# The conditioning vector on the ScalarE queue, and two more k-tiles of q whose shift enters as a bias, in an adaLN transformer block

## The chip, the cores and the metric

The kernel runs on one core of a Trainium2 chip. The metric is device time in microseconds of the whole program, the median of several executions. The profiler's span, which the timelines below use, is 2.2 to 2.6 µs shorter than the device time of the same execution.

## The reference, cut to what matters

```python
# x: [1, 2048, 1024], 32 heads, F = 3584, all bf16
mod = silu(c) @ w_mod                    # six vectors of 1024: sa, ca, ga, sb, cb, gb
h = layernorm(x) * (1 + ca) + sa         # ca: scale, sa: shift
q, k, v = split(h @ wqkv)                # then linear attention, wo, residual with ga
...
h = layernorm(x) * (1 + cb) + sb         # then a SwiGLU block, residual with gb
```

What is changed is only how the first quarter of the rows ("chunk 0": four x tiles of 128 rows) gets from x to q. The contraction over the 1024 input features is done in eight k-tiles of 128.

## The kernel before

The loads are queued on SyncE in the order in which TensorE will want them. `wca` and `wsa` hold the columns of `w_mod` that give the scale and the shift. Each comes in two halves, and half 1 of `wsa` (k-tiles 4 to 7) comes first.

```python
P.dma("c", CS8[0:NDT, :], cv8)                       # 2 KB, queue "sp"
for st in range(4):
    P.dma("x0_%d" % st, XRES[:, st, :], xv[:, st, :])   # x tiles 0..3, 256 KB each
ca_load(0); wq_load(0, 2); ca_load(1); wq_load(2, 2)    # 1 MB, 512 KB, 1 MB, 512 KB
sa_load(1)                                           # 1 MB: shift weights of k-tiles 4..7
wq_load(4); wq_load(5); wq_load(6); wq_load(7)
sa_load(0)                                           # shift weights of k-tiles 0..3
```

The four x tiles are normalised one by one. VectorE takes the statistics of tiles 0, 1 and 3. ScalarE takes those of tile 2, in two passes over it (`act_stats(2)`); `m2` copies them into the form that the rest uses.

```python
act_stats(2)                       # ScalarE: sum, then sum of squares
s0_[0](); s0_[1](); s1_[0](); s0_[2](); ln1_rstd1(0)          # VectorE from here on
s1_[1](); s1_[2](); ln1_rstd1(1)
ln1_xn(0); tile_transposes(0); warm(5, bank=3)
s3_[0]()
ln1_xn_act(1); tile_transposes(1); warm(1, bank=3)            # tile 1 on ScalarE
m2[1](); m2[0](); neg_rstd(2)                                 # needs ScalarE's passes
s3_[1](); s3_[2](); ln1_rstd1(3)
ln1_xn(2); ln1_xn(3)
mod_sc(WCA, 8, range(2)); fin_ca(0, 2); tile_transposes(2, 3)
h0_first(0, "dve"); h0_first(1, "dve")
```

The q projection of chunk 0 keeps seven output tiles (`nt`) open in seven PSUM banks and goes through the k-tiles one or two at a time. K-tiles 0 to 3 get only their scale before the matmul. Their shift enters q as a bias (`bias_mm`: 32 matmuls of one column), and is added to the tiles afterwards, for k. K-tiles 4 to 7 get scale and shift at once, so they need `wsa` first.

```python
mod_sc(WCA, 8, range(4, 8)); fin_ca(4, 4)
for nt in range(7):
    if nt == 6:
        mod_sc(WSA, 0, range(4, 6)); fin_sa(4, 2)     # 16 matmuls: first use of wsa
        for dt in (4, 5): h0_scale(dt)                # VectorE: scale and shift
    q_part(nt, qb[nt], (2, 3))
mod_sc(WSA, 0, range(6, 8)); fin_sa(6, 2)
for dt in (6, 7): h0_scale(dt)
act_stats(4)
for dt in (4, 5, 6):
    for nt in range(7): q_part(nt, qb[nt], (dt,))
... # k-tile 7; between its matmuls mod_sc(WSA, 0, range(4)) and bias_mm()
ln1_xn(5); ln1_xn(4); th_dma(5); th_dma(4)            # chunk 1: normalise, transpose by DMA
... # the eighth output tile
for dt in range(4): h0_shift(dt)
```

Of the kernel before, what the change touches and what calls it, by code (L numbers as in the profile page):

```python
# [93 lines left out]


class _Op:
    __slots__ = ("idx", "eng", "fn", "deps", "signaled", "count", "semkey", "waits", "ninc", "tag")

    def __init__(self, idx, eng, fn, semkey, ninc, tag):
        self.idx = idx  # L100
        self.eng = eng
        self.fn = fn
        self.semkey = semkey
        self.ninc = ninc
        self.deps = {}
        self.signaled = False
        self.count = None
        self.waits = []
        self.tag = tag


def _is_ap(v):
# [6 lines left out]
class _Prog:  # L119
# [7 lines left out]
        self.dma_ops = []  # L127

    def add(self, eng, fn, reads=(), writes=(), lane=None, ninc=1, tag=None):
        if eng in self.COMPUTE:  # L130
            semkey = eng
        else:
            assert lane is not None
            semkey = "lane:" + lane
        op = _Op(len(self.ops), eng, fn, semkey, ninc, tag)
        deps = op.deps

        def deps_add(d):
            if d is op:
                return  # L140
            k = d.semkey
            if k not in deps or deps[k].idx < d.idx:
                deps[k] = d

        banks = set()
        for ap, is_w in [(a, False) for a in reads] + [(a, True) for a in writes]:
            space, ivs = _ap_intervals(ap)
            if space == "dram":
                continue
            if space == "ps":  # L150
                for a, b in ivs:
                    for bank in range(a // PSUM_BANK_BYTES, (b - 1) // PSUM_BANK_BYTES + 1):
                        banks.add(bank)
                continue
            for a, b in ivs:
                self.seg.access(a, b, op, is_w, deps_add)
        for bank in banks:
            st = self.excl.get(bank)
            if st:
                for e2, d in st.items():  # L160
                    if e2 != eng:
                        deps_add(d)
            self.excl[bank] = {eng: op}
        self.ops.append(op)
        self.by_eng.setdefault(eng, []).append(op)
        if eng not in self.COMPUTE:
            self.dma_ops.append(op)
        return op

# [37 lines left out]
    def resolve(self):  # L207
        for op in self.ops:
            for d in op.deps.values():
                d.signaled = True  # L210
        for op in self.ops:
            if op.eng not in self.COMPUTE and op.fn is not None:
                op.signaled = True
        counters = {}
        for op in self.ops:
            if op.signaled:
                c = counters.get(op.semkey, 0) + (op.ninc if op.eng in self.COMPUTE else 16 * op.ninc)
                counters[op.semkey] = c
                op.count = c
        known = {}  # L220
        snaps = {}
        for op in self.ops:
            kn = known.setdefault(op.eng, {})
            waits = []
            for k, d in sorted(op.deps.items(), key=lambda kv: kv[1].idx):
                if kn.get(k, 0) >= d.count:
                    continue
                waits.append((k, d.count))
                for kk, vv in snaps[d.idx].items():
                    if kn.get(kk, 0) < vv:  # L230
                        kn[kk] = vv
                if kn.get(k, 0) < d.count:
                    kn[k] = d.count
            op.waits = waits
            if op.signaled:
                sn = dict(kn)
                if op.eng in self.COMPUTE:
                    sn[op.semkey] = op.count
                snaps[op.idx] = sn
        return counters  # L240

    def emit(self, sems, engines):
        for eng, ops in self.by_eng.items():
            deco = engines[eng]

            def body(e, ops=ops, eng=eng):
                for op in ops:
                    for k, v in op.waits:
                        e.wait_ge(sems[k], v)
                    if op.fn is None:  # L250
                        continue
                    r = op.fn(e)
                    if op.signaled:
                        if eng in self.COMPUTE:
                            r.then_inc(sems[op.semkey], op.ninc)
                        else:
                            rs = r if isinstance(r, (list, tuple)) else [r]
                            assert len(rs) == op.ninc
                            for ri in rs:
                                ri.then_inc(sems[op.semkey], 16)  # L260

            deco(body)


def bass_adaLN_cond__linear_attn_block__swiglu_ffn__prompt_kernel(
# [22 lines left out]
    with ExitStack() as es:  # L288
# [104 lines left out]

        P = _Prog()

        P.dma("c", CS8[0:NDT, :], cv8)
        for st in range(4):
            P.dma("x0_%d" % st, XRES[:, st, :], xv[:, st, :])

# [3 lines left out]
        def sa_load(p):  # L403
            P.dma("wsa%d" % p, WSA[:, :, 512 * p:512 * p + 512], wmv[:, :, 512 * p:512 * p + 512])

        def wq_load(i, n=1):
            P.dma("wq%d" % i, WQK[:, i:i + n, 0:D], wqkvv[:, i:i + n, 0:D])
# [2 lines left out]
        wq_load(0, 2)  # L410
        ca_load(1)
        wq_load(2, 2)
        sa_load(1)
        wq_load(4)
        wq_load(5)
        wq_load(6)
        wq_load(7)
        sa_load(0)
# [97 lines left out]
        def fin_sa(m, n, cast=False):  # L516
            if cast:
                P.dve("tensor_copy", out=MODTMP[:, m:m + n], in_=PS[:, 0, m:m + n])
            P.dve("tensor_copy", out=MODCOL[:, 1, m:m + n], in_=PS[:, 0, m:m + n])

        def h0_shift(dt):
            P.dve("tensor_scalar", out=HT[:, 0, dt, :], in0=HT[:, 0, dt, :], scalar1=MODCOL[:, 1, dt:dt + 1],
                  scalar2=None, op0=ALU.add)

        def bias_mm():
            for nt in range(NDT):
                for dt in range(4):
                    P.pe("matmul", out=PS[:, 0, 16 + nt:17 + nt], lhsT=WQK[:, dt, nt * 128:(nt + 1) * 128],
                         rhs=MODTMP[:, dt:dt + 1], start=False, stop=(dt == 3), skip_group_check=True)
            P.dve("tensor_copy", out=BIASQ[:], in_=PS[:, 0, 16:24])  # L530

        def t_view(dt, n=1):
# [81 lines left out]
        s3_[0]()  # L614
        ln1_xn_act(1)
        tile_transposes(1)
        warm(1, bank=3)
        m2[1]()
        m2[0]()
        neg_rstd(2)  # L620
# [65 lines left out]

        def k_group(ch, nt):
            buf, bank = ch % 2, next_bank()
            for i, dt in enumerate((4, 5, 6, 7, 0, 1, 2, 3) if ch == 0 else range(NDT)):
                P.pe("matmul", out=PS[:, bank, :], lhsT=WQK[:, dt, D + nt * 128:D + (nt + 1) * 128],  # L690
                     rhs=HT[:, buf, dt, :], start=(i == 0), stop=(i == 7))
            phi_evac(bank, (ch, nt))
# [36 lines left out]
        def q_phase_chunk0(side):  # L729
# [9 lines left out]
                    q_part(nt, qb[nt], dts)  # L739
            mod_sc(WCA, 8, range(4, 8))  # L740
            fin_ca(4, 4)
            for nt in range(7):
                if nt == 6:
                    mod_sc(WSA, 0, range(4, 6))
                    fin_sa(4, 2)
                    for dt in (4, 5):
                        h0_scale(dt)
                q_part(nt, qb[nt], (2, 3))
            mod_sc(WSA, 0, range(6, 8))
            fin_sa(6, 2)  # L750
            for dt in (6, 7):
                h0_scale(dt)
            act_stats(4)
            for dt in (4, 5, 6):
                for nt in range(7):
                    q_part(nt, qb[nt], (dt,))
            for nt in range(7):
                if nt == 0:
                    mod_sc(WSA, 0, range(4))
                    fin_sa(0, 4, True)  # L760
                    for f in ln_ops[1]:
                        f()
                    ln1_rstd1(5)
                if nt == 4:
                    bias_mm()
                q_part(nt, qb[nt], (7,))
            for f in act_mv_ops(4):
                f()
            neg_rstd(4)
            ln1_xn(5)  # L770
            ln1_xn(4)
            th_dma(5)
            th_dma(4)
            q_phi = lambda nt: phi_evac(qb[nt] if nt < 7 else 0, PQT[:, nt, 0:512], bias=BIASQ[:, nt:nt + 1])
            for i, dt in enumerate(range(NDT)):
                P.pe("matmul", out=PS[:, 0, :], lhsT=WQK[:, dt, 896:1024], rhs=HT[:, 0, dt, :], start=(i == 0),
                     stop=(i == 7))
            for dt in range(4):
                h0_shift(dt)
            for nt in range(8):  # L780
                q_phi(nt)
                for f in side.get(nt, []):
                    f()
# [389 lines left out]
```

## Time and profile before

| | |
|---|---|
| device time, three runs before the prediction | 836.26, 836.29, 834.89 µs |
| span of the profiled run | 833.0 µs, TensorE busy 99% |
| first projection matmul | 12.67 µs |
| TensorE waits for `wsa` | 0.61 µs, its matmuls start at 20.08 µs |
| first matmul of k | 30.80 µs |

These lines are the head of the page of the kernel before.

```profile
span 833.0 us, 10031 instructions
PE 821.9 (99%) x4053; PEld 379.9 (46%) x4132; DVE 301.7 (36%) x659; ACT 196.2 (24%) x335; POOL 43.6 (5%) x56
PE 94%; DVE 3%; DMA 1%; SPq 1%; issue 1%; ACT 0%; DVEq 0%; ACTq 0%
```

TensorE is the bottleneck. Note 4053 matmuls against 4132 weight loads (PEld): 79 matmul records are missing from this trace. So a milestone of TensorE is read here from the weight loads, which are complete. A weight load is pulled ahead to the start of the matmul before it, so the first matmul starts when the second weight load does. The prediction's 12.88 µs for the first projection matmul is the first matmul record of this trace; by the weight loads it was 12.67.

The chain of waits of the kernel before, in order of time (start, length, what):

```profile
0.79 0.40 SPq L178
1.24 0.36 SPq L178
...
8.79 11.24 DMA wsa<-in_w_mod_dram
20.08 0.57 PE ps L178 x16
...
31.87 10.74 PE ps L178 x49
```

The chain says that nothing before 20.08 µs set the time except the queue of loads that ends in `wsa`.

The next lines are TensorE's timeline of the kernel before (start, length, tiles written and read, count, and in brackets the idle time before it with what ended it). 512-column matmuls start every 0.216 µs, one-column ones every 0.025 µs; the length of a merged line contains the pipeline of its last matmul.

```profile
17.10 2.54 PE L178 MATMUL ps<-ht,wqk 128*128 128x512 bf16 x11
20.08 0.55 PE L178 MATMUL ps<-siluc,wsa 128*128 128x1 bf16 x16 [0.44 <-DMA wsa<-in_w_mod_dram]
20.50 0.59 PE L178 MATMUL ps<-ht,wqk 128*128 128x512 bf16 x2
20.93 0.54 PE L178 MATMUL ps<-siluc,wsa 128*128 128x1 bf16 x16
...
27.62 0.94 PE L178 MATMUL ps<-modtmp,wqk 128*128 128x1 bf16 x32
```

The last matmul ahead of `wsa` starts at 19.26 µs, so the next could have started at 19.48; it starts at 20.08. Measured from start to start the wait is 0.61 µs; the 0.44 in the bracket leaves out the pipeline's drain. "Wait" below is start to start beyond the 0.216 µs pace.

Two views of the fill belong together. First ScalarE's timeline, then VectorE's, both of the kernel before.

```profile
6.28 1.06 ACT L178 ACTIVATE ht<-xres 128x1024 bf16<-128x1024 bf16 x1 [3.68 <-DMA xres<-in_A_x_dram]
7.24 0.19 ACT L178 ACTIVATION_READ_ACCUMULATOR ht<-xres 128x1 f32 x1
7.46 1.06 ACT L178 ACTIVATE ht<-xres 128x1024 bf16<-128x1024 bf16 x1
8.42 0.19 ACT L178 ACTIVATION_READ_ACCUMULATOR ht<-xres 128x1 f32 x1
```

```profile
7.21 0.54 DVE L178 TENSOR_SCALAR xres<-xres,mv,rstd 128x1024 bf16<-128x1024 bf16 x1
7.82 0.69 DVE L178 BATCH_NORM_STATS2 stats<-xres 128x6 f32<-128x512 bf16 x1
8.43 0.20 DVE L178 TENSOR_SCALAR nmr<-mv,rstd 128x1 f32<-128x1 f32 x1
8.64 0.22 DVE L178 SCALAR_TENSOR_TENSOR mv<-sumx,sumsq 128x1 f32<-128x1 f32 x1
```

The statistics at 7.82 start 0.02 µs after x tile 3 has landed (7.80), 0.61 µs behind the operation ahead of them. Short waits got no bracket in VectorE's timeline. From its first statistics (4.03) to the operation at 8.64, VectorE took 4.61 µs here.

### The profile page before, as it was taken

The page shows a single profiled execution, that of the slowest core. Times are in us where ns is not written, and L with a number is a line of the kernel's source. Part 1 is how long each engine was busy: PE and PEld are TensorE (multiplying, and loading weights), DVE is VectorE, ACT ScalarE, POOL GpSimd, SP SyncE. Part 2 cuts the span into 40 slices and gives each one's busy share as a digit, 9 for nine tenths or more (in the row PEclk, how much of TensorE's full clock was granted, in tenths as well). Part 3 has the DMA queues.
Part 4 walks back from the last instruction along what each step waited for, and adds up shares of the span by engine and source line. Part 5 has one row for each costly group of instructions (what it writes and reads, how often), then busy time and mean ns, then how long its engine had stood idle before and what let it go on. Part 6 is the DMA issues. An engine that isn't in the chain of part 4 may idle for free.

```text
span 833.0 us, 10031 instructions
## 1 busy us (share of the span) xinstructions
PE 821.9 (99%) x4053; PEld 379.9 (46%) x4132; DVE 301.7 (36%) x659; ACT 196.2 (24%) x335; POOL 43.6 (5%) x56
## 2 busy tenths in 40 slices
PE   7999999999999999999999999999999999999998
PEld 4544444454444444444444444444444444444444
DVE  5797985657873211110222211122111212111111
ACT  3667642223332111110211111111111111111011
POOL 1000000000050000030000003000000300000000
PEclk9999999999999999999999999999999999999999
DMA  9969734928197995610455571045557004553000
GB/s 312 298 149 228 205 74 146 200 103 303 34 222 241 255 272 152 177 51 13 114 152 152 151 186 42 13 113 153 152 152 198 28 13 119 152 154 93 1 26 25
DMA packets 190940, 117.17 MB, mean 141 GB/s; under 512 B 49576, under 2 KB 174640, under 8 KB 190896
## 3 DMA queue, kind: packets, MB, share of 16 engines
q1 hardware_dynamic: 190896, 116.55, 50.7%
q8 instruction: 32, 0.52, 0.3%
q14 instruction: 12, 0.10, 0.0%
HBM read 100.67 MB, written 4.33 MB: 126 GB/s over the span
## 4 chain that ended last, share of the span: by engine, by line
PE 94%; DVE 3%; DMA 1%; SPq 1%; issue 1%; ACT 0%; DVEq 0%; ACTq 0%
PE ps L178 94%; DMA wsa<-in_w_mod_dram 1%; DVE acc L178 1%; SPq L178 1%; DVE xres L178 0%; DVE pkt L178 0%; DVE mhl L178 0%; DVE ht L178 0%; DVE e L178 0%; DVE pqt L178 0%; ACT e L178 0%; ACT mw L178 0%; DVE ve L178 0%; DVE modcol L178 0%; DVE ut L178 0%
## 5 line engine op out<-in xcount | busy, mean ns | idle before, releaser
L178 PE MATMUL ps<-h2t,guu 128*128 128x512 bf16 x878 | 210.1, 379 | 0.9
L178 PE MATMUL ps<-h2t,gug 128*128 128x512 bf16 x878 | 209.9, 379 | 0.9
L178 DVE TENSOR_TENSOR at<-sg,ps 128x512 bf16<-128x512 bf16 x112 | 77.0, 687 | 296.2 <-PE ps L178 285.1
L178 ACT ACTIVATE sg<-ps 128x512 bf16<-128x512 f32 x112 | 66.9, 597 | 310.3 <-PE ps L178 298.9
L178 PEld LDWEIGHTS ps<-h2t,guu 128*128 128x128 bf16 x896 | 87.7, 98 | 105.7
L178 PEld LDWEIGHTS ps<-h2t,gug 128*128 128x128 bf16 x896 | 87.5, 98 | 105.3
L178 PE MATMUL ps<-wd_a,at 128*128 128x512 bf16 (+2 forms) x519 | 112.8, 372 | 0.5
L178 PE MATMUL ps<-ht,wqk 128*128 128x512 bf16 x498 | 110.7, 379 | 1.0 <-DVE ht L178 0.3
L178 PE MATMUL ps<-wd_b,at 128*128 128x512 bf16 (+2 forms) x388 | 85.4, 372 | 0.5
L178 PEld LDWEIGHTS ps<-wd_a,at 128*128 128x128 bf16 x528 | 51.1, 98 | 59.8
L178 PEld LDWEIGHTS ps<-ht,wqk 128*128 128x128 bf16 x512 | 49.3, 98 | 58.7 <-DVE mv L178 0.3
L178 DVE TENSOR_TENSOR ut<-att,gb_b 128x512 bf16<-128x512 bf16 (+1 forms) x32 | 13.8, 432 | 167.3 <-ACT att L178 167.3
L178 ACT ACTIVATE att<-ps 128x512 bf16<-128x512 f32 (+1 forms) x32 | 17.4, 591 | 182.1 <-PE ps L178 182.1
L178 PEld LDWEIGHTS ps<-wd_b,at 128*128 128x128 bf16 x396 | 38.3, 98 | 44.6
L178 PE MATMUL ps<-pk,xres 128*128 128x512 bf16 x250 | 56.2, 379 | 0.4 <-issue 0.2
L178 PE MATMUL ps<-mw,pqt 128*128 128x512 bf16 x250 | 55.8, 379 | 0.4
L178 POOL TENSOR_SCALAR h2t<-h2t,modcol 128x512 bf16<-128x512 bf16 x32 | 28.6, 912 | 394.9 <-DMA h2t<-xn 378.6
L178 ACT ACTIVATE e<-ps 128x512 bf16<-128x512 f32 x56 | 33.0, 602 | 32.8 <-PE ps L178 27.3
L178 PEld LDWEIGHTS ps<-mw,pqt 128*128 128x128 bf16 x256 | 24.9, 98 | 29.7 <-DVE xres L178 0.2
L178 PEld LDWEIGHTS ps<-pk,xres 128*128 128x128 bf16 x256 | 24.8, 98 | 29.8 <-issue 0.4
L178 ACT ACTIVATE junk<-xres 128x1024 bf16<-128x1024 bf16 x24 | 25.4, 1059 | 36.0 <-DVE xres L178 35.8
L178 POOL TENSOR_TENSOR rstd<-ve,neghalf 128x1 f32<-128x1 f32 (+2 forms) x17 | 14.2, 850 | 215.7 <-DVE ve L178 176.4
(101 smaller groups left out, 342.5 us busy)
## 6 DMA issues: line engine op xcount, KB each, us to landing
gug<-in_B_w_gate_dram SPq DMA_DIRECT2D x56, 512.0 KB, 4.0
guu<-in_B_w_up_dram SPq DMA_DIRECT2D x56, 512.0 KB, 5.3
xres<-in_A_x_dram SPq DMA_DIRECT2D x20, 256.0 KB, 8.0
rb<-recip_den SPq DMA_DIRECT2D x8, 512.0 KB, 11.9
stgx<-in_w_mod_dram SPq DMA_DIRECT2D x2, 2048.0 KB, 8.8
wd_a<-in_B_w_down_dram SPq DMA_DIRECT2D x4, 1024.0 KB, 7.5
out_dram<-xres SPq DMA_DIRECT2D x31, 128.0 KB, 1.7
xres<-in_A_x_dram SPq DMA_DIRECT2D x3, 1024.0 KB, 14.5
```

The lines of the kernel that those rows point to most:

```text
L178: return getattr(e, method)(**kw)
```

## The change

The intent: x is issued sooner, because c leaves SyncE's queue for ScalarE's; and TensorE has more to do before it needs `wsa`, because k-tiles 4 and 5 no longer need their shift before their matmuls. For that, their weights are loaded ahead of `wsa`. VectorE's order of shifts follows. The core of the diff, without the bookkeeping that lets a compute engine issue a DMA. Also left out: the k-tile order of k and of the eighth output tile is changed to match, and the `wsa` matmuls of k-tiles 0 to 3 come one output tile later:

```diff
-        P.dma("c", CS8[0:NDT, :], cv8)
+        P.dma("c", CS8[0:NDT, :], cv8, queue="act")
...
         wq_load(2, 2)
+        wq_load(4, 2)
         sa_load(1)
-        wq_load(4)
-        wq_load(5)
         wq_load(6)
...
-        warm(1, bank=3)
+        warm(0, bank=3)
...
+            for dt in (4, 5):
+                h0_scale_only(dt)
             for nt in range(7):
-                if nt == 6:
-                    mod_sc(WSA, 0, range(4, 6)) ...   # and h0_scale of 4, 5
-                q_part(nt, qb[nt], (2, 3))
-            mod_sc(WSA, 0, range(6, 8)) ...           # and h0_scale of 6, 7
+                q_part(nt, qb[nt], (2, 3))
+            act_stats(4)
+            for nt in range(7):
+                if nt == 4:
+                    mod_sc(WSA, 0, range(6, 8)) ...   # and h0_scale of 6, 7
+                q_part(nt, qb[nt], (4, 5))
+            mod_sc(WSA, 0, range(4, 6))
+            fin_sa(4, 2, True)
             for nt in range(7):
+                if nt == 2:
+                    bias_mm((4, 5))                   # 16 more one-column matmuls
+                q_part(nt, qb[nt], (6,))
...
+            for dt in (4, 5):
+                h0_shift(dt)
+            ln1_xn(5)
+            th_dma(5)
             for dt in range(4):
                 h0_shift(dt)
+            ln1_xn(4)
+            th_dma(4)
```

More of the change, by code (lines that the diff above doesn't have):

```diff
@@ L96 @@
 class _Op:
-    __slots__ = ("idx", "eng", "fn", "deps", "signaled", "count", "semkey", "waits", "ninc", "tag")
+    __slots__ = ("idx", "eng", "fn", "deps", "signaled", "count", "semkey", "waits", "ninc", "tag", "isdma")
     def __init__(self, idx, eng, fn, semkey, ninc, tag):
@@ L109, in __init__ @@
         self.tag = tag
+        self.isdma = semkey.startswith("lane:")
 def _is_ap(v):
@@ L129, in add @@
     def add(self, eng, fn, reads=(), writes=(), lane=None, ninc=1, tag=None):
-        if eng in self.COMPUTE:
-            semkey = eng
-        else:
-            assert lane is not None
-            semkey = "lane:" + lane
+        semkey = eng if lane is None else "lane:" + lane
+        assert eng in self.COMPUTE or lane is not None
         op = _Op(len(self.ops), eng, fn, semkey, ninc, tag)
@@ L165, in add @@
         self.by_eng.setdefault(eng, []).append(op)
-        if eng not in self.COMPUTE:
+        if op.isdma:
             self.dma_ops.append(op)
@@ L211, in resolve @@
         for op in self.ops:
-            if op.eng not in self.COMPUTE and op.fn is not None:
+            if op.isdma and op.fn is not None:
                 op.signaled = True
@@ L216, in resolve @@
             if op.signaled:
-                c = counters.get(op.semkey, 0) + (op.ninc if op.eng in self.COMPUTE else 16 * op.ninc)
+                c = counters.get(op.semkey, 0) + (16 * op.ninc if op.isdma else op.ninc)
                 counters[op.semkey] = c
@@ L236, in resolve @@
                 sn = dict(kn)
-                if op.eng in self.COMPUTE:
+                if not op.isdma:
                     sn[op.semkey] = op.count
@@ L253, in body @@
                     if op.signaled:
-                        if eng in self.COMPUTE:
+                        if not op.isdma:
                             r.then_inc(sems[op.semkey], op.ninc)
@@ L519, in fin_sa, with h0_scale_only @@
             P.dve("tensor_copy", out=MODCOL[:, 1, m:m + n], in_=PS[:, 0, m:m + n])
+        def h0_scale_only(dt):
+            P.dve("tensor_scalar", out=HT[:, 0, dt, :], in0=HT[:, 1, dt, :], scalar1=MODCOL[:, 0, dt:dt + 1],
+                  scalar2=None, op0=ALU.mult)
         def h0_shift(dt):
@@ L523, in h0_shift, with bias_mm, bias_fin @@
                   scalar2=None, op0=ALU.add)
-        def bias_mm():
+        def bias_mm(dts):
             for nt in range(NDT):
-                for dt in range(4):
+                for dt in dts:
                     P.pe("matmul", out=PS[:, 0, 16 + nt:17 + nt], lhsT=WQK[:, dt, nt * 128:(nt + 1) * 128],
                          rhs=MODTMP[:, dt:dt + 1], start=False, stop=(dt == 3), skip_group_check=True)
+        def bias_fin():
             P.dve("tensor_copy", out=BIASQ[:], in_=PS[:, 0, 16:24])
@@ L688, in k_group @@
             buf, bank = ch % 2, next_bank()
-            for i, dt in enumerate((4, 5, 6, 7, 0, 1, 2, 3) if ch == 0 else range(NDT)):
+            for i, dt in enumerate((6, 7, 4, 5, 0, 1, 2, 3) if ch == 0 else range(NDT)):
                 P.pe("matmul", out=PS[:, bank, :], lhsT=WQK[:, dt, D + nt * 128:D + (nt + 1) * 128],
@@ L741, in q_phase_chunk0 @@
             fin_ca(4, 4)
+            for dt in (4, 5):
+                h0_scale_only(dt)
             for nt in range(7):
-                if nt == 6:
-                    mod_sc(WSA, 0, range(4, 6))
-                    fin_sa(4, 2)
-                    for dt in (4, 5):
-                        h0_scale(dt)
-                q_part(nt, qb[nt], (2, 3))
-            mod_sc(WSA, 0, range(6, 8))
-            fin_sa(6, 2)
-            for dt in (6, 7):
-                h0_scale(dt)
-            act_stats(4)
-            for dt in (4, 5, 6):
-                for nt in range(7):
-                    q_part(nt, qb[nt], (dt,))
-            for nt in range(7):
-                if nt == 0:
+                q_part(nt, qb[nt], (2, 3))
+            act_stats(4)
+            for nt in range(7):
+                if nt == 4:
+                    mod_sc(WSA, 0, range(6, 8))
+                    fin_sa(6, 2)
+                    for dt in (6, 7):
+                        h0_scale(dt)
+                q_part(nt, qb[nt], (4, 5))
+            mod_sc(WSA, 0, range(4, 6))
+            fin_sa(4, 2, True)
+            for nt in range(7):
+                if nt == 2:
+                    bias_mm((4, 5))
+                q_part(nt, qb[nt], (6,))
+            for nt in range(7):
+                if nt == 1:
                     mod_sc(WSA, 0, range(4))
                     fin_sa(0, 4, True)
-                    for f in ln_ops[1]:
-                        f()
-                    ln1_rstd1(5)
+                    ln_ops[1][0]()
+                    ln_ops[1][1]()
                 if nt == 4:
-                    bias_mm()
+                    bias_mm(range(4))
+                    bias_fin()
                 q_part(nt, qb[nt], (7,))
+            ln_ops[1][2]()
+            ln1_rstd1(5)
             for f in act_mv_ops(4):
@@ L769, in q_phase_chunk0 @@
             neg_rstd(4)
-            ln1_xn(5)
-            ln1_xn(4)
-            th_dma(5)
-            th_dma(4)
             q_phi = lambda nt: phi_evac(qb[nt] if nt < 7 else 0, PQT[:, nt, 0:512], bias=BIASQ[:, nt:nt + 1])
-            for i, dt in enumerate(range(NDT)):
+            for i, dt in enumerate((4, 5, 0, 1, 2, 3, 6, 7)):
                 P.pe("matmul", out=PS[:, 0, :], lhsT=WQK[:, dt, 896:1024], rhs=HT[:, 0, dt, :], start=(i == 0),
                      stop=(i == 7))
+            for dt in (4, 5):
+                h0_shift(dt)
+            ln1_xn(5)
+            th_dma(5)
             for dt in range(4):
                 h0_shift(dt)
+            ln1_xn(4)
+            th_dma(4)
             for nt in range(8):
```

## The prediction

> **What bounds the kernel now.** TensorE. The busy table gives PE 821.9 of the 833.0 us span (99%); the chain of waits puts 94% on PE; the granted clock is 1.0. A 128x512 matmul starts every 0.216 us. The timeline's start-to-start gaps leave some 4.6 us beyond that pace. What this change can touch lies in the first 31 us: the fill up to the first projection matmul (12.88 us), and one stall of 0.61 us, where TensorE has run ahead of the second half of the shift weights (wsa): they landed at 20.03 us. The chain of waits shows the same: SyncE issue from 0.79 us, the wsa DMA from 8.79 to 20.03, then PE without a break.
>
> **The fill.** x tile 0 is issued at 1.24 us, because the 2 KB vector c goes first at 0.79; it lands at 4.03. From there VectorE's timeline is almost solid to 11.53 us, then transposes, scaling at 12.04, first matmul at 12.88. So the fill moves with x.
>
> **What changes, and its cost.**
> 1. c on the ScalarE queue: every SyncE issue starts 0.45 us earlier (1.24 - 0.79), and landings move with it. c still lands near 2.2 us. The Trainium skill ("DMA: Bandwidth & Descriptors", Issuing engines are not separate DMA queues) says that another issuing engine only saves sequencer time; this trace agrees, at 0.45 us. Its "ScalarE: Activation LUTs" (What ACT_TABLE_LOAD costs) puts the table load before its ACTIVATE, at 1.28 us, the duration here too; behind c's issue it should end near 2.5 us, about when SiLU runs now (2.42). On the path: -0.45 us.
> 2. k-tiles 4, 5 of wq before wsa, and q over 2 to 5 before the first wsa matmul: wsa comes 1.4 us later (512 KB at the DMA view's 370 GB/s) less 0.45, near 21.0 us; TensorE arrives ten matmuls later (2.16 us) less 0.45, near 21.2. The stall goes. On the path: -0.6 us.
> 3. Bias for tiles 4, 5: 16 more one-column matmuls at 0.025 us: +0.40 us. Two matmuls cover the wait for VectorE's two small copies; I estimate 0.1 us of stall. On the path: +0.5 us.
> 4. The warm-up matmul removed (0.22 us) stands before a wait for wca: worth nothing.
> 5. VectorE: two shifts added (0.28 us each, from four in 1.13). Tile 4's normalisation and transpose move behind six shifts, some 1.3 us later. Chunk 1's modulated tiles come near 42.4 us in place of 42.05, for a use near 44: off the path.
>
> Sum: -0.45 - 0.6 + 0.5 = -0.55 us. First k matmul: 30.80 us now, near 30.25 after. Everything later is the same work at the same pace.
>
> **Prediction: 835.7 us, range 834.3 to 836.9.** Three runs of before differ by 1.4 us, more than the effect. Chances: faster by over 2% 0.005, within 2% 0.99, slower 0.005.
>
> **What would show it.** x tile 0's DMA issued near 0.8 us, landing near 3.6; first projection matmul near 12.4; no gap before the wsa matmuls; 48 bias matmuls, not 32; first k matmul 30.1 to 30.5; span 832.3 to 832.7.
>
> **What would make it wrong.** The table load running before c's issue: c would land near 3.5 us and hold the warm-up matmuls and VectorE's SiLU copy, which stand before everything else. x not moving with its issue. wsa, or its first half (due near 25.3 us, needed near 25.5), landing late. TensorE's clock dropping in the gap before the first projection. Chunk 1's transposes coming 1.5 us later than thought, which would stall TensorE at 44 us.

## The result, and the profile after

| | runs | median | range |
|---|---|---|---|
| before, the first comparison | 4 | 835.62 µs | 834.89 to 836.29 |
| after, the first comparison | 4 | 834.46 µs | 834.35 to 835.14 |
| before, all sessions | 34 | 835.16 µs (mean 835.26) | 834.48 to 836.46 |
| after, all sessions | 9 | 834.69 µs (mean 834.81) | 834.30 to 835.82 |

The ratio of the first comparison is 0.9988, with a 95% interval of 0.9971 to 1.0005: the same, within what the runs can tell. A ratio here is the mean time of one kernel's fast runs over that of the other's of the same rounds, so it isn't quite the ratio of the medians. Over all sessions the means differ by 0.45 µs, with an uncertainty of about 0.4 (two standard errors, from standard deviations of 0.45 and 0.51 µs). Predicted were 835.7 µs and a difference of 0.55 µs.

The head of the page after:

```profile
span 832.1 us, 10139 instructions
PE 825.8 (99%) x4147; PEld 380.1 (46%) x4147; DVE 302.8 (36%) x662; ACT 196.3 (24%) x335; POOL 43.2 (5%) x56
PE 97%; DVE 2%; DMA 0%; issue 0%; POOL 0%; ACT 0%; DVEq 0%
```

TensorE's busy time seems to have grown by 3.9 µs; 79 of the 94 further matmul records are those that the first trace lacked. The 15 more weight loads are the true difference (16 bias matmuls more, one warm-up less).

The chain of waits after, from its start:

```profile
0.79 2.81 DMA xres<-in_A_x_dram
3.60 0.03 issue
3.62 1.88 DVE stats L176 x3
...
7.89 0.11 DVE nmr L176
8.00 0.20 DVE mv L176 x2
```

`wsa` has left the chain. It now starts with x tile 0 and goes through VectorE's statistics. But the step at 8.00 is a near tie. VectorE's timeline after:

```profile
7.80 0.20 DVE L176 TENSOR_SCALAR nmr<-mv,rstd 128x1 f32<-128x1 f32 x1
7.92 0.22 DVE L176 SCALAR_TENSOR_TENSOR mv<-sumx,sumsq 128x1 f32<-128x1 f32 x1
```

The operation at 7.92 starts 0.03 µs after ScalarE's second pass over x tile 2 has ended (7.89), as it did before, and also 4.30 µs after VectorE's first statistics (3.62), its pace without waits. The chain view shows only one of the two paths.

TensorE's timeline after, the lines that answer to those of before:

```profile
16.17 4.91 PE L176 MATMUL ps<-ht,wqk 128*128 128x512 bf16 x22
20.92 0.54 PE L176 MATMUL ps<-siluc,wsa 128*128 128x1 bf16 x16
21.32 1.46 PE L176 MATMUL ps<-ht,wqk 128*128 128x512 bf16 x6
...
23.02 0.59 PE L176 MATMUL ps<-ht,wqk 128*128 128x512 bf16 x2
23.54 0.55 PE L176 MATMUL ps<-modtmp,wqk 128*128 128x1 bf16 x16
...
26.70 0.94 PE L176 MATMUL ps<-modtmp,wqk 128*128 128x1 bf16 x32
```

22 matmuls stand ahead of `wsa` in place of 12, and the bracket is gone. There are 16 new bias matmuls at 23.54 µs. And ScalarE's timeline after:

```profile
0.79 0.58 ACTq L176 DMA_DIRECT2D cs<-in_c_dram  x1
1.41 1.28 ACT L176 ACT_TABLE_LOAD   x1 [1.41 <-PEq L1168]
2.70 0.18 ACT L176 ACTIVATE siluc<-ps 128x8 bf16<-128x8 bf16 x1
5.56 1.06 ACT L176 ACTIVATE ht<-xres 128x1024 bf16<-128x1024 bf16 x1 [2.68 <-DMA xres<-in_A_x_dram]
```

c is issued first on ScalarE and the table load follows it. SiLU runs 0.28 µs later than before (2.42). VectorE waits 0.21 µs for its result (a cast at 2.91), but not on the path: x tile 0 lands at 3.60.

Between these two profiles the balance up to the first matmul of k is:

| | µs |
|---|---|
| first projection matmul 12.67 to 11.95 | -0.72 |
| wait for `wsa` 0.61 to 0 | -0.61 |
| a small wait after the second `wsa` group, gone | -0.10 |
| 16 bias matmuls, 16 x 0.025 | +0.40 |
| waiting for VectorE's copies before them | +0.09 |
| sum; first k matmul 30.80 to 29.87 | -0.93 |

It explains this pair in full (span 833.05 to 832.13). But it is one pair of profiles, and 0.72 and 0.61 µs are larger than the time that the medians of all runs show. The experiments ask which of these numbers are the change and which are chance.

### The profile page after: what moved, and what is told of

The parts are those of the page before. It is cut to its first block, busy times and chain, and to the rows that moved or that the text cites. A ratio compares the mean times of both kernels' runs of the same rounds, so it can differ in the third digit from the quotient of the medians.

```text
span 832.1 us, 10139 instructions
## 1 busy us (share of the span) xinstructions
PE 825.8 (99%) x4147; PEld 380.1 (46%) x4147; DVE 302.8 (36%) x662; ACT 196.3 (24%) x335; POOL 43.2 (5%) x56
## 4 chain that ended last, share of the span: by engine, by line
PE 97%; DVE 2%; DMA 0%; issue 0%; POOL 0%; ACT 0%; DVEq 0%
PE ps L176 97%; DVE stats L176 0%; DVE xres L176 0%; DMA xres<-in_A_x_dram 0%; DVE acc L176 0%; DVE mhl L176 0%; DVE ve L176 0%; POOL rstd L176 0%; DVE mv L176 0%; ACT mw L176 0%; DVE ut L176 0%; DVE mean L176 0%; DVE msq L176 0%; DVE nmr L176 0%; DVE sumx L176 0%
## 5 line engine op out<-in xcount | busy, mean ns | idle before, releaser
L176 PEld LDWEIGHTS ps<-wd_b,at 128*128 128x128 bf16 x396 | 38.3, 98 | 44.7
## 6 DMA issues: line engine op xcount, KB each, us to landing
rb<-recip_den SPq DMA_DIRECT2D x8, 512.0 KB, 11.9
```

The costliest lines, as they stand in the source:

```text
L176: return getattr(e, method)(**kw)
```

## The experiments

All twelve ran in three sessions beside the kernel before. "Tile 2" is the landing of x tile 2, when the last of its 16 DMA engines has reported; the semaphore records of the trace show each report. "First q" is the first projection matmul.

| profile | tile 2 | first q | difference | first `wsa` matmul | wait there | span |
|---|---|---|---|---|---|---|
| before | 6.25 | 12.67 | 6.42 | 20.08 | 0.61 | 833.05 |
| before_again | 6.09 | 12.51 | 6.42 | 19.61 | 0.29 | 832.59 |
| load_order_only | 6.06 | 12.48 | 6.42 | 20.75 | 1.47 | 833.73 |
| c_only | 5.46 | 11.97 | 6.51 | 19.53 | 0.75 | 832.50 |
| after | 5.54 | 11.95 | 6.41 | 20.92 | 0 | 832.13 |
| after_again | 5.93 | 12.34 | 6.41 | 21.60 | 0.29 | 833.02 |
| k_only | 5.84 | 12.25 | 6.41 | 21.22 | 0 | 832.46 |
| no_bias45 | 5.77 | 12.18 | 6.41 | 21.15 | 0 | 832.37 |
| warm_back | 5.92 | 12.34 | 6.42 | 21.58 | 0.28 | 832.89 |
| tile2_later | 4.89 | 11.84 | 6.95 | 20.80 | 0 | 832.01 |
| third_pass | 5.67 | 13.27 | 7.60 | 22.23 | 0 | 833.45 |
| swap23 | 6.62 | 13.03 | 6.41 | 22.00 | 0 | 833.21 |
| swap23_later | 6.65 | 12.42 | 5.77 | 21.39 | 0 | 832.68 |
| polished | 5.43 | 11.75 | 6.32 | 21.15 | 0 | 832.24 |

### First session: is the fill's gain the change or chance, and do the parts add up?

**The kernel before, again.** No edit.

> The kernel before, unchanged, looked at a second time: the null. Ratio to before within 0.999 to 1.001. Theory A (the spread between the fastest and the slowest of the 16 DMA engines comes from c standing at the head of SyncE's queue): x tile 3's first engine lands near 5.5 us and its last near 7.8 us again, a spread over 1.8 us; tile 2 lands near 6.25, first projection matmul near 12.67. Theory B (the spread is chance, run by run): the last engine of tile 3 lands anywhere between 6.2 and 7.8 us, and the first projection matmul moves with it by up to 0.3 us.

Measured: 835.29 µs median of 5, ratio 1.0001 (0.9988 to 1.0013). Tile 3's engines landed from 5.655 to 6.814 µs, a spread of 1.16 µs; in the first profile they landed from 5.49 to 7.80, a spread of 2.31. The wait for `wsa` was 0.29 µs, half of what the first profile had. Theory A (c's place makes the spread) expected over 1.8 µs and misses.

**The changed kernel, again.** No edit.

> The changed kernel, unchanged, a second time. Ratio to before 0.9985 to 0.9992 (0.7 to 1.2 us less). Theory A: tile 3's engines again within 0.9 us of one another, last near 6.2 us; first projection matmul at 11.95 +- 0.05. Theory B: spread anywhere between 0.7 and 2.3 us, first matmul up to 12.2 us.

Measured: 834.79 µs median of 5 (834.30 to 835.82), ratio 0.9997 (0.9985 to 1.0010), where 0.9985 to 0.9992 was expected. First q came at 12.34 µs, 0.39 later than in the first profile, with tile 2's landing at 5.93 in place of 5.54. `wsa` landed at 21.56 µs in place of 19.94, and 0.29 µs of waiting for it was back. The profiled span was 833.02, longer than that of the kernel before in the same session. The fastest engine reports for `wsa` at 18.34 and 18.56 µs in the two profiles; the slowest at 19.94 and 21.56. So what varies is mostly the slowest engine. Theory A is out.

**Only c moved.**

```diff
# kernel before
-        P.dma("c", CS8[0:NDT, :], cv8)
+        P.dma("c", CS8[0:NDT, :], cv8, queue="act")
```

> The kernel before with only c moved to the ScalarE queue. Both theories: x tile 0 issued at 0.79 us and landed near 3.6. Theory A: first projection matmul near 11.95 us (0.72 us less than before), engines of tile 3 within 0.9 us. wsa also lands earlier (near 18.5 us by its narrower spread, against 20.04), TensorE arrives near 18.75 us, so the 0.61 us stall is gone without any other part of the change: span 831.6 to 831.8, better than the whole change. Theory B with a wide spread: first matmul near 12.2, wsa near 19.6, stall 0.6 stays, span near 832.5. My prediction's own sum (0.45 us for c and nothing else) says 832.55.

Measured: 834.48 µs median of 5 (834.33 to 835.12), ratio 0.9992 (0.9979 to 1.0006). First q came at 11.97, as the whole change had it. Yet `wsa` landed at 19.48, so its matmul started at 19.53 after a wait of 0.75 µs, and the span was 832.50. The first profile's 0.70 µs of fill became 0.55 µs of span, because TensorE, sooner at the same gate, waited longer. TensorE's timeline of this run:

```profile
16.41 2.54 PE L176 MATMUL ps<-ht,wqk 128*128 128x512 bf16 x11
19.53 0.55 PE L176 MATMUL ps<-siluc,wsa 128*128 128x1 bf16 x16 [0.59 <-DMA wsa<-in_w_mod_dram]
```

**Everything but c.**

```diff
# changed kernel
-        P.dma("c", CS8[0:NDT, :], cv8, queue="act")
+        P.dma("c", CS8[0:NDT, :], cv8)
```

> The changed kernel with c put back as the first transfer of the SyncE queue: k-tiles, loads, bias and VectorE order as changed. Theory A: x's spread is that of before (tile 3 last near 7.8 us), first projection matmul near 12.67; no wait for wsa (lands near 21.4, TensorE arrives near 21.6) or a small one; 16 more bias matmuls cost 0.40 and 0.09 us: span 832.7 to 833.0, within 0.3 us of before. Theory B: spread by chance, span between 832.3 and 833.0. If the parts add up, this gain and that of c_only sum to the whole's 0.93 only if the wsa stall isn't counted twice.

Measured: 835.09 µs median of 5, ratio 0.9998 (0.9986 to 1.0011), span 832.46, no wait for `wsa`, tile 3's spread 1.23 µs with c at the head of SyncE's queue again. That is theory B's range. The interval of each of these ratios holds 1, so the times alone rank nothing. In particular, the record doesn't show that moving the k-tiles adds anything to moving c: in these same five rounds the means were 835.21 µs for the kernel before, 834.62 with c alone, 835.08 with everything but c, and 834.97 with the whole change, with standard deviations of 0.3 to 0.6. The profiles show which wait held.

What follows is a rule for each order of TensorE. With the order of before, four profiles have the span 812.97 or 812.98 µs after the first `wsa` matmul, whatever the fill did (833.05 - 20.08, 832.59 - 19.61, 832.50 - 19.53 and, below, 833.73 - 20.75). With the changed order and no wait for `wsa`, the span is 820.17 to 820.26 µs after first q in six profiles (for example 832.13 - 11.95 and 832.46 - 12.25). So the landing of `wsa` sets the time before, and the fill sets it after, when `wsa` comes in time.

### Second session: what binds the fill, what the bias costs, what the load order does

**A third statistics pass on ScalarE.**

```diff
# changed kernel, after act_stats(2)
+        P.act("activation", out=HT[:, 1, 0:2, :], in_=..., func=ACT.Square,
+              scale=D ** -0.5, accum_out=SUMSQ[:, 2:3])
```

> The changed kernel with the second of ScalarE's two statistics passes over x tile 2 run twice (same numbers, 1.18 us more of ScalarE). Six profiles have the first projection matmul 6.41 to 6.51 us after tile 2's last landing. Theory A (tile 2's landing and ScalarE's statistics bind the fill): first matmul 7.5 to 7.6 us after tile 2's landing, near 13.1 to 13.5 us; span 833.2 to 833.8. Theory B, my prediction's (x tile 0 and VectorE's solid chain bind it): first matmul near 12.0 us whatever ScalarE does, span near 832.2. The wait for wsa should be gone under A (TensorE comes later, wsa does not).

Measured: 835.86 µs median of 4, ratio 1.0007 (0.9992 to 1.0021). First q came 7.60 µs after tile 2's landing in place of 6.41: ScalarE's added 1.18 µs went through to TensorE undiminished. ScalarE's timeline shows the three passes and then, without a bracket, tile 1's normalisation, which in the changed kernel had waited 0.23 µs for VectorE. The delay of tile 1 isn't what TensorE saw: its wait in the transposes of tiles 2 and 3, 0.71 µs up to 12.18, is for VectorE. VectorE's line, below those of ScalarE, shows VectorE waiting for the third pass:

```profile
6.88 1.06 ACT L176 ACTIVATE ht<-xres 128x1024 bf16<-128x1024 bf16 x1
...
8.06 1.06 ACT L176 ACTIVATE ht<-xres 128x1024 bf16<-128x1024 bf16 x1
9.02 0.19 ACT L176 ACTIVATION_READ_ACCUMULATOR ht<-xres 128x1 f32 x1
9.11 1.22 ACT L176 ACTIVATE xres<-xres,nmr,rstd 128x1024 bf16<-128x1024 bf16 x1
```

```profile
9.24 0.22 DVE L176 SCALAR_TENSOR_TENSOR mv<-sumx,sumsq 128x1 f32<-128x1 f32 x1 [1.32 <-ACT ht L176]
```

The prediction's reading (x tile 0, then VectorE) said near 12.0 µs; it came at 13.27.

**Tile 3's second statistics ahead of tile 2's small operations.**

```diff
# changed kernel
+        s3_[1]()
         m2[1](); m2[0](); neg_rstd(2)
-        s3_[1]()
         s3_[2]()
```

> The changed kernel with tile 3's second statistics put ahead of the four small operations that need tile 2's, on VectorE only. Theory A: the first matmul no longer follows tile 2's landing: 12.05 +- 0.1 us for a landing anywhere between 5.4 and 6.1 us (changed kernel: landing + 6.41, so 11.95 to 12.5). Theory B: no difference, near 11.95 to 12.35 as in the two profiles of the changed kernel.

Measured: 834.32 µs median of 4 (834.21 to 834.85), ratio 0.9990 (0.9975 to 1.0005); first q 11.84 µs. Inconclusive: tile 2 happened to land at 4.89 µs in this profile, so early that neither order would have waited for it. The third session forces it late.

**Without the bias matmuls of k-tiles 4 and 5,** a result that lacks a part of the shift. (It still passed the comparison with the reference, whose tolerance doesn't see this term.)

```diff
# changed kernel
-                if nt == 2:
-                    bias_mm((4, 5))
```

> The changed kernel without the 16 bias matmuls of k-tiles 4 and 5: WRONG RESULT ON PURPOSE (q lacks a part of the shift). In the changed kernel the span is the first projection matmul plus 820.2 us when no wait for wsa is left. If the bias costs what I sized, 0.40 us of matmuls and 0.09 of waiting for VectorE's copies, it is plus 819.7 here. If those matmuls were free (hidden behind other waits), plus 820.2 stays.

Measured: 834.20 µs median of 4, ratio 0.9986 (0.9969 to 1.0003). The span was first q plus 820.19, not 819.7: a miss. The 16 matmuls and their 0.09 µs of waiting are gone from the timeline, so their size was right. But TensorE then came 0.48 µs too soon for the other half of `wsa`, whose last engine reported at 25.40 µs:

```profile
23.46 1.67 PE L176 MATMUL ps<-ht,wqk 128*128 128x512 bf16 x7
25.45 0.95 PE L176 MATMUL ps<-siluc,wsa 128*128 128x1 bf16 x32 [0.32 <-DMA wsa<-in_w_mod_dram]
```

A cost of 0.49 µs was taken away and a new wait took 0.48 of it back. There is a second gate, 4.3 µs behind the first. The first gate's margin isn't all there is.

**Only the load order.**

```diff
# kernel before
+        wq_load(4, 2)
         sa_load(1)
-        wq_load(4)
-        wq_load(5)
```

> The kernel before with wq tiles 4 and 5 loaded ahead of wsa and nothing else; TensorE's order unchanged. Three profiles with TensorE's order of before have span = start of the first wsa matmul + 812.97, whatever the fill did, so the wsa landing alone sets the time. Theory A: wsa 1.4 us later, landing 20.9 to 21.5 us, wait of 1.6 to 2.2 us before its first matmul, span again start of the first wsa matmul + 812.97, 833.9 to 834.5. If the load order itself were worth something, the span would stay below 833.

Measured: 836.51 µs median of 4 (836.03 to 840.00), ratio 1.0024 (1.0003 to 1.0044). One run of 840.00, with a granted clock of 0.996, lies apart from the other three and raises the ratio, but each of the other three (836.03 to 836.77) is also longer than every run of the kernel before that was timed beside them (834.48 to 835.92). The wait grew to 1.47 µs, less than expected because `wsa` landed at 20.70, a little before the 20.9 that I had set as the low end. The span was again the first `wsa` matmul plus 812.98 µs. So the load order without TensorE's new order is a loss; it is the price that TensorE's order pays for.

### Third session: the binding tile forced late, the warm-up matmul, and a mended version

**x tile 3 loaded ahead of tile 2.**

```diff
# changed kernel
-        for st in range(4):
+        for st in (0, 1, 3, 2):
```

> The changed kernel with x tile 3 loaded ahead of tile 2, so tile 2 lands last, near 6.2 to 6.7 us. Theory A (tile 2's statistics on ScalarE bind the fill): first projection matmul = tile 2's landing + 6.41, 12.6 to 13.1 us, 0.4 to 0.9 us later than in the changed kernel. Theory B (my prediction's: tile 0 and VectorE): near 12.0.

Measured: 835.59 µs median of 4, ratio 1.0005 (0.9991 to 1.0019). First q came at 13.03 µs = 6.62 + 6.41. With the landing late, VectorE's wait is long enough for a bracket:

```profile
7.67 0.20 DVE L176 TENSOR_SCALAR nmr<-mv,rstd 128x1 f32<-128x1 f32 x1
9.01 0.22 DVE L176 SCALAR_TENSOR_TENSOR mv<-sumx,sumsq 128x1 f32<-128x1 f32 x1 [1.13 <-ACT ht L176]
```

**The same, with tile 3's second statistics first** (the edit of the second session added).

> The same swapped loads, with tile 3's second statistics ahead of tile 2's small operations on VectorE. Theory A: the first matmul comes tile 2's landing + 5.8 +- 0.15 us, so 0.5 to 0.6 us sooner than the swapped loads alone. If that order on VectorE is worth nothing, + 6.41 as in the kernel with swapped loads alone.

Measured: 835.01 µs median of 4, ratio 0.9999 (0.9985 to 1.0013). Tile 2 landed at 6.65, first q came at 12.42, 5.77 after it: 0.64 µs less. VectorE's timeline shows why. The statistics, 0.61 µs of VectorE, now lie inside the wait:

```profile
7.75 0.68 DVE L176 BATCH_NORM_STATS2 stats<-xres 128x6 f32<-128x512 bf16 x1
9.04 0.22 DVE L176 SCALAR_TENSOR_TENSOR mv<-sumx,sumsq 128x1 f32<-128x1 f32 x1 [0.61 <-ACT ht L176]
```

So a late tile 2 binds the fill, through ScalarE's two passes. It is VectorE's in-order queue that turned them into a wait for everything behind.

The prediction's path is the second gate, and a close one. In VectorE's given order, tile 2's first small operation (`mv<-sumx,sumsq`) starts 2.39 µs after tile 2's landing, or 4.32 µs after tile 0's landing, whichever is later; with two passes on ScalarE this holds to within 0.01 µs in all ten profiles. So tile 2 binds when it lands more than 1.93 µs after tile 0 (an estimate, the difference of these two figures). With c alone moved it landed 1.82 µs after, and tile 0 with VectorE's work bound; in the first profile of the changed kernel it was 1.94, a tie; in the other seven profiles with x in its usual order it was 1.97 to 2.45.

**The warm-up matmul put back.**

```diff
# changed kernel
-        warm(0, bank=3)
+        warm(1, bank=3)
```

> The changed kernel with the removed warm-up matmul (0.22 us) put back. It stands between tile 1's transposes and the wca matmuls, ahead of a wait of 0.3 to 0.7 us for tile 3: worth nothing, first projection matmul again tile 2's landing + 6.41 us (or 11.95 when that is less). If it were on the path: + 6.6.

Measured: 834.69 µs median of 4, ratio 0.9994 (0.9981 to 1.0008), first q 6.42 µs after tile 2's landing. Worth nothing, as predicted.

**Four orders mended at once.**

```diff
# changed kernel, with tile 3's second statistics first
-                if nt == 4:                            # first wsa matmuls
+                if nt == 5:
-                if nt == 2:                            # bias of k-tiles 4, 5
+                if nt == 4:
...
             ln1_xn(5); th_dma(5)
+            ln1_xn(4); th_dma(4)
             for dt in range(4): h0_shift(dt)
-            ln1_xn(4); th_dma(4)
```

> The changed kernel with four orders mended: tile 3's second statistics ahead of tile 2's small operations; the first wsa matmuls one output tile later (0.43 us more room for wsa); the bias matmuls of tiles 4, 5 two matmuls later (0.09 us of waiting for VectorE's copies gone); tile 4's normalisation and transpose ahead of the four shifts again. Theory A (what is left are waits for late DMA engines): span = first projection matmul + 820.1 us in nearly every run, first matmul near 11.9 to 12.1, span 831.9 to 832.3, 0.2 to 0.7 us less than the changed kernel on average, with a smaller spread of runs. Theory B (chance alone makes the differences): mean as the changed kernel's, 834.8.

Measured: 834.45 µs median of 5 (mean 834.43, 833.98 to 835.01), ratio 0.9990 (0.9977 to 1.0004). First q 11.75 µs (11.9 to 12.1 was expected), no wait at the first gate, no wait before the new bias matmuls. But the span was first q plus 820.49: 0.12 µs of waiting at the second `wsa` gate, and 0.19 µs at 44.7 µs, where chunk 1 begins. Its mean is the lowest of the correct kernels timed in five rounds, 0.38 µs under the changed kernel's over all sessions. But the two were never in the same rounds, and 0.38 is less than the standard deviation of the changed kernel's runs (0.51). The kernel with the first of the four orders alone has the same mean, 834.43 µs over four runs of the second session. That the mended version is better isn't shown.

### The wait at chunk 1

The profile of the changed kernel's second look had one more wait, at 45.1 to 45.8 µs. TensorE's weight loads there:

```profile
45.10 0.10 PEld L176 LDWEIGHTS ps<-ht,wqk 128*128 128x128 bf16 x1 [0.16 <-DVE ht L176]
45.42 0.10 PEld L176 LDWEIGHTS ps<-ht,wqk 128*128 128x128 bf16 x1 [0.23 <-DVE ht L176]
```

The brackets hold the usual idle time between weight loads too; beyond TensorE's pace the matmuls lost 0.15 µs here in all. The kernel with the swapped loads and tile 3 first lost 0.06 at this place, the one with the warm-up matmul put back 0.04.

VectorE modulates chunk 1's eight k-tiles in one row, after the last DMA transpose has landed. These are its lines in the kernel before, in the changed kernel and in the changed kernel's second look:

```profile
42.05 2.67 DVE L178 TENSOR_SCALAR ht<-ht,modcol 128x512 bf16<-128x512 bf16 x8 [0.36 <-DMA ht<-xres]
```

```profile
42.33 2.67 DVE L176 TENSOR_SCALAR ht<-ht,modcol 128x512 bf16<-128x512 bf16 x8 [1.30 <-DMA ht<-xres]
```

```profile
43.35 2.67 DVE L176 TENSOR_SCALAR ht<-ht,modcol 128x512 bf16<-128x512 bf16 x8 [1.48 <-DMA ht<-xres]
```

VectorE makes a tile every 0.33 µs (2.67/8) and TensorE uses one every 0.216, so the last tile counts, not the first. TensorE wants it 13.81 + 1.51 µs after the first k matmul (64 and 7 matmuls). That is 46.12 µs before, against 44.72 when it is ready: 1.40 µs of room. In the changed kernel it is 45.19 against 45.00: 0.19 µs. In its second look it is 45.92 against 46.02, and TensorE waits.

The transposes themselves changed. From issue to landing, the third of chunk 1's four transposes took 3.2 to 3.3 µs in all four profiles with VectorE's old order, and 4.5 to 4.8 in nine of ten with the new (the tenth, without the bias matmuls, took 3.2). Loads and transposes around it are the same in number. Putting tile 4's normalisation forward again (the mended version) didn't bring the short time back (4.8).

The DMA packets of the traces show what goes with it. In all nine long cases a 16 KB packet of the kind `instruction` starts while the third transpose is under way (38.69 to 40.32 µs), and more than 20 of the packets in that stretch take over 1 µs each (the longest 1.24 to 1.76). In all five short cases that packet starts only after 42 µs, when the third and the fourth transpose have landed, and no packet of the third takes over 0.12 µs. The changed kernel has 15 matmuls more than the kernel before, the one without the bias matmuls one fewer, so the programs' instructions lie differently. That is an agreement in 14 profiles of 14; no run moves the fetch alone, so that it is the cause isn't shown.

## Why the prediction was right or wrong

The time, 834.46 µs, lies in the predicted range (834.3 to 836.9), and the difference over all sessions, 0.45 µs, fits the predicted 0.55. The sum came out right; one of its steps was read wrongly, and one addition isn't one. That the time lies in the range is in part luck. The 835.7 was counted from the median of three runs of the kernel before, 836.26, and two of these three are longer than all but one of the other 31 runs. The time is 0.16 µs above the range's lower end. And three marks of "What would show it" missed in the first pair: first q came at 11.95 µs (near 12.4), the first k matmul at 29.87 (30.1 to 30.5), the span was 832.13 (832.3 to 832.7).

1. **"c on the ScalarE queue ... On the path: -0.45 us."** The issue moved as said (x tile 0 from 1.24 to 0.79 µs), and the table load followed c as said. The size is right on average: tile 2 landed at 6.06 µs in the mean of four profiles with c first on SyncE (5.84 to 6.25), and at 5.58 in the mean of eight with c on ScalarE and x in its usual order (4.89 to 5.93), 0.48 less, with an uncertainty of about 0.3 (two standard errors). The way was only half right. **"From there VectorE's timeline is almost solid ... So the fill moves with x"**, with tile 0 meant: tile 2, through ScalarE, sets first q (landing + 6.41 to 6.42 µs) in nine profiles out of nine with VectorE's given order, ScalarE's two passes and a landing over 5.5 µs. The third pass and the two swapped kernels show it. In one of the nine, the first profile of the changed kernel, tile 0's path ends at the same time; with c alone moved (landing 5.46) it ends last, as the prediction had it. In the first pair of profiles the term measured 0.72, since the slowest DMA engine happened to be early in one and late in the other.
2. **"The stall goes. On the path: -0.6 us."** It was gone in eight of the ten profiles with TensorE's new order; in two there was one of 0.28 to 0.29 µs, as `wsa` landed after 21.5 µs where I had said 21.0. The 0.61 was itself one draw: the kernel before showed 0.29 the next time. A further 0.10 µs, the small wait after the second `wsa` group, also went; the prediction didn't have it.
3. **The sum of 1 and 2.** With the old order of TensorE the landing of `wsa` sets the time and c's gain can come only from an earlier `wsa`. With the new order the fill sets it. The two terms aren't independent: first q 0.70 µs sooner with c alone met a wait of 0.75 µs. I wrote them as a plain sum, which is right only if `wsa` moves as far as x.
4. **"+0.40 us ... 0.1 us of stall."** Right: 16 matmuls at 0.025 µs, and 0.09 µs. What I hadn't seen is that taking this cost away needn't pay, since the second gate stands behind it.
5. **"worth nothing"** for the warm-up matmul: right.
6. **"near 42.4 us in place of 42.05, for a use near 44: off the path."** The first number is right (42.33), by luck. The prediction delayed tile 4's transpose; in fact it was issued at 32.20 µs in place of 33.74 and landed at 38.16 in place of 38.93. What came late were the third and the fourth transpose, which took 4.5 and 4.1 µs in place of 3.2 each. The conclusion was too easy: I compared the first tile with the first use. By the last tile only 0.19 µs of room was left.

Shown by the runs: what binds the fill, the rule for each order, the bias's size, the loss from the load order alone. Open: whether the k-tiles' move gains anything beyond c's, which DMA engine is slow and why, whether the instruction packet is what makes the transpose long, and whether the mended version is truly faster.

## What to carry to other kernels

A gap's end is set by whatever comes last, so gains ahead of a gate don't add to gains at it. Write the time as "gate + rest" for each candidate gate, and see which one held in several profiles before summing. When an effect is under 0.1%, profile the unchanged kernel twice first. And in an in-order queue, put an operation that waits for another engine behind work that doesn't; a timeline that looks solid may hide short waits.

## What the Trainium skill lacked or had wrong

- "DMA: Bandwidth & Descriptors" (Latency and other measured facts) says that two of the engines are usually slower than the others, as its best guess for loads that GpSimd issues only, and gives no size. The loads here are issued by SyncE, and the 16 engines' reports for the fourth 256 KB x tile lay 0.76 to 2.31 µs apart, differently in two executions of the same kernel (2.31 and 1.16 before, 0.76 and 1.32 after), and the lag was carried on to the loads behind (1.6 to 3.0 µs for `wsa` in the changed kernel). The traces don't name the engine.
- The same page (Issuing engines are not separate DMA queues) says that another issuing engine only saves the time on the sequencer. This held: 0.45 µs. It doesn't say that the time to issue differs: the same 2 KB load took 0.40 µs on SyncE and 0.58 on ScalarE.
- The same page (DMA Transpose) gives no duration, and no page says that an instruction packet can go with a longer one: the same transpose took 3.2 to 3.3 µs from issue to landing in five profiles, and 4.5 to 4.8 in the nine in which a 16 KB `instruction` packet fell into it.
- "ScalarE: Activation LUTs" (What ACT_TABLE_LOAD costs) agrees on the load itself: 1.28 µs here, placed behind the DMA issue (that the load stands before its ACTIVATE is said on the same page under "Step-by-step: what each stage is for"). The section adds a drain and gives about 2.66 µs in all for every switch to another set. No drain shows here: in the kernel before, ScalarE's second load follows an operation that ends at 13.65 µs, starts at 13.67, and the next operation starts at 14.96, so 1.31 µs in all.
- "TensorE: Matmul & The Clock Gate" (Wait — 56ns, not 53.3ns?) agrees: 0.025 µs from one one-column matmul to the next, 0.216 for 512 columns.
